# kv of six batches on two column halves of the matmul array, one head each, and one more batch's x on quarters

## The chip, the cores and the metric

One core of one Trainium2 chip runs the whole kernel. The metric is the device time of one execution in microseconds (us); lower is better. "Span" is the time from the first to the last instruction in a profile; it is some 1.8 us shorter than the device time.

Names as in the profile: PE is TensorE's matmuls, PEld its weight loads, DVE is VectorE, ACT is ScalarE, POOL is GpSimd. Of the program's names, pskv is the result of kv, psx and psxr are those of x (512 positions, and the other 64), psg and psv those of the up-projection (gate and value), psy that of the down-projection; xt and xtr are the copies of x, and ht the gated product, that the next matmuls read; yo is the output before it is stored.

## The reference

Linear attention over 8 batches, 8 heads, 576 positions, head size 64, followed by a gated feed-forward block over the 4608 tokens:

```python
q_s = softmax(q, axis=-1)                       # over the head dimension
k_s = softmax(k, axis=2)                        # over the sequence
kv  = np.einsum('bhsd,bhse->bhde', k_s, v)      # 64 x 64 per head
x   = np.einsum('bhsd,bhde->bhse', q_s, kv)     # then heads side by side: (4608, 512)
g   = x @ w_gate                                # 512 -> 1536
out = (gelu(g) * (x @ w_val)) @ w_out           # 1536 -> 512
```

Inputs and output are float32. The kernel computes in float16 with float32 sums.

## The kernel before

The feed-forward matmuls of one batch run on TensorE while the other engines prepare the next batch's attention. The small attention matmuls are slipped between the feed-forward matmuls by a plan: `at(b, FI, i, ...)` runs something after the i-th of twelve up-projection steps of batch b, and `at(b, NS, i, ...)` in its down-projection (0 to 3: after one of the four row blocks; 10 to 13: in the middle of one).

kv is computed for two heads at once on the whole array: the stationary weights are 128 columns of exp(k) (two heads), and the moving operand is v of the same two heads, each with a column of ones behind it (130 columns; the ones give the softmax sum). Half of the 128 x 130 result belongs to mismatched heads and is masked to zero:

```python
def kv_mm(b, g, j):
    ...
    hp = 2 * g + j
    for n in range(NC):                                            # NC = 5 chunks of positions
        nc.tensor.matmul(
            st[(b, "pskv", g)][:, j, :], ek_b[b % 2][:, n, hp * P:(hp + 1) * P],
            v16_b[b % 2][:, n, 2 * hp:2 * hp + 2, 0:VW],           # VW = 65
            start=(n == 0), stop=(n == NC - 1))

def kv_norm(b, g):
    pskv = st[(b, "pskv", g)]
    rck = att.tile([P, 2], f32, name="rck", tag="rck")
    nc.vector.reciprocal(out=rck, in_=pskv[:, :, D])
    for j in range(2):
        kv_sb = att.tile([P, 2, D], f16, name="kv_sb", tag="kv", bufs=12)
        nc.vector.scalar_tensor_tensor(                            # times 1/sum, times the mask
            out=kv_sb, in0=..., scalar=rck[:, j:j + 1], in1=mask, op0=ALU.mult, op1=ALU.mult)

def unit_kv(b, g):
    kv_mm(b, g, 0)
    kv_mm(b, g, 1)
    kv_norm(b, g)
```

For batches 3 to 7, x = q kv already runs on four 64x64 quarters of the array (`unit_x4`: row half s is one head's kv, column half t one of two head pairs). That needs heads h and h+4 side by side, which `exp` and `cast_v` arrange for batches from `T32 = 3` on. Batch 2 still uses the whole array (`unit_x`, four matmuls, and `unit_xrem`). The plan:

```python
at(1, NS, 0, L(unit_trem, 2), L(unit_kv, 2, 0))
at(1, NS, 1, L(unit_x, 2, 0, "dve"))
at(1, NS, 12, L(unit_kv, 2, 1))
at(1, NS, 2, L(unit_x, 2, 1, "dve"), L(unit_x, 2, 2, "dve"))
at(1, NS, 13, L(unit_x, 2, 3, "act"))
at(2, FI, 0, L(unit_xrem, 2, "dve"))
...
for b in range(2, B):                      # n = b + 1, batches 3 to 7
    ...
    at(b, FI, 5, L(unit_kv, n, 0))
    at(b, FI, 7, L(unit_kv, n, 1))
    at(b, NS, 1, L(unit_x4, n))
```

The softmax here doesn't subtract the row's maximum and nothing guards it: scores larger than these inputs give would overflow.

Of the kernel before, what the change touches and what calls it, by code (L numbers as in the profile page):

```python
# [9 lines left out]
f32 = mybir.dt.float32  # L10
f16 = mybir.dt.float16
ACTF = mybir.ActivationFunctionType
ALU = mybir.AluOpType
# [5 lines left out]
def kernel(  # L19
# [10 lines left out]
    nc = tc.nc  # L30

    B, H, S, D = q.shape
    C = H * D
    F = moe_w_gate.shape[1]
    P = 128
    HP = H // 2
# [6 lines left out]
    NC = NM + 1  # L43
    MAIN = NM * P
    REM = S - MAIN
    VW = D + 1
# [7 lines left out]
    att = ctx.enter_context(tc.tile_pool(name="att", bufs=2))  # L54
# [4 lines left out]
    ps_att = ctx.enter_context(tc.tile_pool(name="ps_att", bufs=2, space=bass.MemoryType.PSUM))  # L59
# [9 lines left out]
    ek_b, eq_b, v16_b = [], [], []  # L69
# [30 lines left out]



    T32 = 3

    def heads(x, b, h0, h1):

        if b >= T32:
            return x.rearrange("p (t c) x -> p c t x", t=2)[:, h0 // 2:h1 // 2]
        return x[:, h0:h1]

    tiles = {}
# [24 lines left out]
    def copy_on(eng, dst, src):  # L136
        if eng == "pool":
            nc.gpsimd.tensor_copy(out=dst, in_=src)  # L138
        elif eng == "act":
            nc.scalar.copy(out=dst, in_=src)  # L140
        else:
            nc.vector.tensor_copy(out=dst, in_=src)  # L142
# [14 lines left out]

    def exp(nm, b, h0=0, h1=H, n0=0):
        dst = (ek_b if nm == "k" else eq_b)[b % 2]
        o, i = (("p n (c t d) -> p c t n d", "p c t (n d) -> p c t n d") if b >= T32 else  # L160
                ("p n (h d) -> p h n d", "p h (n d) -> p h n d"))
        nc.scalar.activation(  # L162
            out=dst[:, n0:NC, h0 * D:h1 * D].rearrange(o, d=D, **({"t": 2} if b >= T32 else {})),
            in_=heads(tiles[(nm, b)], b, h0, h1)[..., n0 * D:NC * D].rearrange(i, d=D),
            func=ACTF.Exp)

    def cast_v(b, h0, h1, eng="pool"):
        if h1 - h0 > 2 and (eng == "pool" or b >= T32):
            for h in range(h0, h1, 2):
                cast_v(b, h, h + 2, eng)  # L170
            return
        copy_on(eng, v16_b[b % 2][:, :, h0:h1, 0:D].rearrange("p n h d -> p h n d"),
                (tiles[("v", b)][:, h0 // 2::4] if b >= T32 else tiles[("v", b)][:, h0:h1]).rearrange(
                    "p h (n d) -> p h n d", d=D))

    def norm_sum(b, hp, n0=0):
# [42 lines left out]
    st = {}  # L219
# [11 lines left out]
# [6 lines that stand above are left out]
            nc.vector.scalar_tensor_tensor(  # L237
                out=kv_sb,
                in0=pskv[:, j, :].rearrange("p (h e) -> p h e", e=VW)[:, :, 0:D],
                scalar=rck[:, j:j + 1], in1=mask, op0=ALU.mult, op1=ALU.mult)  # L240
            st[(b, "kv", 2 * g + j)] = kv_sb
# [29 lines left out]
    def unit_kv(b, g):  # L271
        kv_mm(b, g, 0)
        kv_mm(b, g, 1)
        kv_norm(b, g)

    def get_eqt(b):
        if (b, "eqt") not in st:
            st[(b, "eqt")] = att.tile([P, HP * 4 * NC * 32], f16, name="eqt", tag="eqt")[
                :, 0:HP * S].rearrange("p (h t) -> p h t", h=HP)
        return st[(b, "eqt")]  # L280

    def unit_t(b, g, eng="dve"):
        eqt = get_eqt(b)
        pst = ps_att.tile([P, 2, MAIN], f16, name="pst", tag="att")
        for j in range(2):
            hp = 2 * g + j
            for n in range(NM):
                nc.tensor.transpose(  # L288
                    pst[:, j, n * P:(n + 1) * P],
                    eq_b[b % 2][:, n + 1, hp * P:(hp + 1) * P], ident)  # L290
        st["evac_t"] = lambda eng: copy_on(eng, eqt[:, 2 * g:2 * g + 2, 0:MAIN], pst)
        if eng:
            st["evac_t"](eng)
# [33 lines left out]
    def xq(b, hp):  # L327

        if (b, "eqt5") in st:
            return st[(b, "eqt5")][:, hp, 1:NC]  # L330
        return st[(b, "eqt")][:, hp, 0:MAIN]

    def xqr(b, hp):
        if (b, "eqt5") in st:
            return st[(b, "eqt5")][:, hp, 0, :, 0:32:2]
        return st[(b, "eqtr")][:, hp, :]

    def get_xt(b):
        if (b, "xt") not in st:
            st[(b, "xt")] = att.tile([P, HP, MAIN], f16, name="xt", tag="xt")  # L340
        return st[(b, "xt")]
# [13 lines left out]
                             xqr(b, hp), start=True, stop=True)  # L355
        copy_on(eng, xtr[:, :, b * REM:(b + 1) * REM], psx)

    def unit_x4(b):

        xt = get_xt(b)  # L360

        def go(ps, hp, src):
            for s in range(2):
                r, t = slice(64 * s, 64 * s + 64), hp % 2
                nc.tensor.matmul(ps[s][64 * t:64 * t + 64], st[(b, "kv", hp)][r, s, :], src[r],  # L365
                                 start=True, stop=True)

        psr = [ps_att.tile([P, 2, REM], f32, name="psxr", tag="att") for _ in range(2)]
        for hp in range(HP):
            go([p[:, hp // 2] for p in psr], hp, xqr(b, hp))  # L370
        for s, eng in enumerate(("act", "dve")):
            copy_on(eng, xtr[:, 2 * s:2 * s + 2, b * REM:(b + 1) * REM], psr[s])
        for i in range(2):
            ps = [ps_big.tile([P, MAIN], f32, name="psx", tag="mm") for _ in range(2)]
            for hp in (2 * i, 2 * i + 1):
                go(ps, hp, xq(b, hp))
            for s, eng in enumerate(("act", "dve")):
                copy_on(eng, xt[:, i + 2 * s, :], ps[s])

    pswarm = ps_big.tile([P, 512], f32, name="pswarm", tag="mm")  # L380
# [160 lines left out]

    preload(ACTF.Exp)
    exp("q", 0, 0, 4, 1)
    exp("q", 0, 4, 8, 1)
    exp("k", 0, 0, 4)
    exp("k", 0, 4, 8)
    norm_pair(0, 0, 1, ("dve", "pool"))
# [7 lines left out]
    warm_pe(2)  # L555
    ksum_mm((2, 3))
    cast_v(0, 0, 2, "dve")
    cast_v(0, 2, 4, "act")
    ksum_rec()
    cast_v(0, 4, 6, "act")  # L560
    kv0_mm(0)
    kv0_mm(1)
# [23 lines left out]
    FI, NS = 0, 1  # L586
    plan = {}

    def at(b, kind, i, *fns):
        plan.setdefault((b, kind, i), []).extend(fns)  # L590

    L = lambda f, *a: (lambda: f(*a))
# [25 lines left out]
    at(1, FI, 9, L(unit_t, 2, 0))  # L618
    at(1, FI, 10, L(unit_t, 2, 1))
    at(1, FI, 11, L(load_batch, 3), L(exp, "k", 2, 4, 8), L(exp, "q", 3), L(exp, "k", 3), L(exp_rem0), L(cast_v, 3, 0, H))  # L620
    at(1, NS, 0, L(unit_trem, 2), L(unit_kv, 2, 0))
    at(1, NS, 1, L(unit_x, 2, 0, "dve"))
    at(1, NS, 12, L(unit_kv, 2, 1))
    at(1, NS, 2, L(unit_x, 2, 1, "dve"), L(unit_x, 2, 2, "dve"))
    at(1, NS, 13, L(unit_x, 2, 3, "act"))
    at(2, FI, 0, L(unit_xrem, 2, "dve"))
    at(2, FI, 7, L(norm_rem0))
    at(3, FI, 8, L(unit_trem, 0))
    at(3, FI, 11, L(unit_xrem, 0, "dve"))
    for b in range(2, B):  # L630
        if b + 2 < B:
            at(b, FI, 0, L(load_batch, b + 2))
            at(b, FI, NFI - 1, L(exp, "q", b + 2), L(exp, "k", b + 2), L(cast_v, b + 2, 0, H))
        if b + 1 < B:
            n = b + 1
            if n < T32:
                at(b, FI, 0, L(norm, n, 0))
                at(b, FI, 1, L(unit_kv, n, 0))
                at(b, FI, 2, L(norm, n, 1))
                at(b, FI, 3, L(unit_kv, n, 1))  # L640
                at(b, FI, 4, L(unit_t, n, 0), L(norm, n, 2))
                at(b, FI, 6, L(unit_x, n, 0), L(norm, n, 3))
                at(b, FI, 7, L(unit_x, n, 1))
                at(b, FI, 8, L(unit_t, n, 1))
                at(b, FI, 9, L(unit_trem, n))
                at(b, FI, 10, L(unit_x, n, 2), L(unit_x, n, 3))
                at(b, FI, 11, L(unit_xrem, n))
            else:
                for hp in range(HP):
                    at(b - 1, NS, hp, L(norm_sum, n, hp))  # L650
                    at(b, FI, hp, L(norm_mul, n, hp), L(unit_t32, n, hp))
                at(b, FI, 4, L(moves, n))
                at(b, FI, 5, L(unit_kv, n, 0))
                at(b, FI, 7, L(unit_kv, n, 1))
                at(b, NS, 1, L(unit_x4, n))


    def ride(b, kind, i):
# [68 lines left out]
```

## Time and profile before

| | before |
|---|---|
| device time, median (range) | 318.7 us (318.4 to 318.91, 3 runs) |
| span of the profiled run | 316.7 us |
| TensorE busy | 98% of the span |
| VectorE, ScalarE, GpSimd busy | 62%, 44%, 14% |
| kv matmuls on the whole array (L226) | 2% of the chain that ended last |

The busy shares say which engine can be the bound, not that it is. The chain of work that ended last and the waits say that. The prediction below shows these views and reads them. In all of them L226 is the source line; in a timeline line the first two numbers are start and duration in us, and the end of the line has the shape and the count. Durations of matmuls are modelled and overlap; only starts are used here.

### The profile page before, as it was taken

How to read it: one execution, taken by the hardware profiler on the slowest of the kernel's cores; microseconds unless marked ns; L12 is line 12 of the kernel's file. 1: busy time of each engine (PE TensorE's matmuls, PEld its weight loads, DVE VectorE, ACT ScalarE, POOL GpSimd, SP SyncE). 2: the span in 40 equal slices, each digit the busy share in tenths (PEclk: the TensorE clock that was granted, in tenths of full speed). 3: DMA queues.
4: the chain of work that ended last, by engine and by line, in shares of the span. 5: the costliest groups of instructions: out<-in, count | busy, mean ns of one | idle time of the engine just before them, and what ended most of it. 6: DMA issues, size and time to landing. Idle time of an engine off the chain costs nothing.

```text
span 316.7 us, 4572 instructions
## 1 busy us (share of the span) xinstructions
PE 309.7 (98%) x1698; PEld 146.8 (46%) x1698; DVE 195.4 (62%) x346; ACT 138.4 (44%) x179; POOL 44.6 (14%) x59
## 2 busy tenths in 40 slices
PE   8799999999999999999999999999999999999995
PEld 3444454455445444544444444444444444444444
DVE  3843386698898479847884689458953434234331
ACT  3753465989433663258233923392331233113300
POOL 2657551331003000110003000300000000000000
PEclk9999999999999999999999999999999999999999
DMA  7999999940196117821592149303020210140002
GB/s 229 372 383 395 400 386 388 394 174 0 68 321 236 45 66 251 291 56 68 169 364 63 55 122 382 97 10 132 3 63 23 91 42 2 27 105 2 2 33 99
DMA packets 42342, 50.76 MB, mean 160 GB/s; under 512 B 3408, under 2 KB 38096, under 8 KB 42320
## 3 DMA queue, kind: packets, MB, share of 16 engines
q1 hardware_dynamic: 40592, 48.84, 44.5%
q10 hardware_dynamic: 1728, 1.64, 1.6%
q8 instruction: 13, 0.21, 0.3%
q14 instruction: 9, 0.07, 0.1%
HBM read 37.75 MB, written 9.44 MB: 149 GB/s over the span
## 4 chain that ended last, share of the span: by engine, by line
PE 90%; DMA 4%; ACT 3%; DVE 2%; issue 1%; ACTq 0%
PE psy L471 29%; PE psg L393 28%; PE psv L393 28%; PE pskv L226 2%; DMA out_dram<-yo 2%; DMA qt<-in_q_dram 2%; PE psl L492 1%; DVE rq L190 1%; PE psx L365 1%; PE psx L347 1%; ACT eq L162 1%; PE pst L288 1%; DVE eq L199 0%; ACT L398 0%; ACT L162 0%
## 5 line engine op out<-in xcount | busy, mean ns | idle before, releaser
L398 ACT ACTIVATE gl<-psg 128x512 f32<-128x512 f32 x108 | 63.9, 598 | 141.4 <-PE psg L393 138.6
L400 DVE SCALAR_TENSOR_TENSOR ht<-psv,gl 128x512 f16<-128x512 f32 x108 | 72.9, 682 | 63.6 <-PE psv L393 63.0
L393 PE MATMUL psg<-xt,wg_sb 128*128 128x512 f16 x384 | 100.5, 379 | 0.1
L393 PE MATMUL psv<-xt,wv_sb 128*128 128x512 f16 x384 | 100.5, 379 | 0.0
L471 PE MATMUL psy<-wo_sb,ht 128*128 128x512 f16 x420 | 94.3, 379 | 0.0
L393 PEld LDWEIGHTS <-wv_sb 128*128 128x128 f16 x432 | 42.3, 98 | 51.2 <-issue 0.8
L393 PEld LDWEIGHTS <-wg_sb 128*128 128x128 f16 x432 | 41.6, 98 | 47.0 <-issue 0.4
L471 PEld LDWEIGHTS <-ht 128*128 128x128 f16 x420 | 40.4, 98 | 49.2 <-issue 2.1
L520 DVE TENSOR_SCALAR yo<-psy 128x512 f32<-128x512 f32 x30 | 20.6, 688 | 29.0 <-PE psy L471 29.0
L138 POOL CAST v<-vt 128x640 f16<-128x640 f32 x26 | 18.7, 761 | 137.5 <-DMA vt<-in_v_dram 92.2
L180 DVE TENSOR_REDUCE rq<-eq 128x10 f32<-128x640 f16 x28 | 22.7, 811 | 5.5 <-ACT eq L162 5.1
L199 DVE TENSOR_TENSOR eq<-eq,rrq 128x640 f16<-128x640 f16 (+1 forms) x29 | 23.4, 806 | 0.3
L162 ACT ACTIVATE ek<-kt 128x1280 f16<-128x1280 f32 (+1 forms) x11 | 19.1, 1746 | 3.4 <-DMA kt<-in_k_dram 3.4
L162 ACT ACTIVATE eq<-qt 128x2560 f16<-128x2560 f32 (+2 forms) x10 | 18.4, 1863 | 2.4 <-DMA qt<-in_q_dram 2.3
L313 DVE STREAM_TRANSPOSE et<-eq 128x640 f16<-128x640 f16 x20 | 16.9, 845 | 0.7
L140 ACT CAST xt<-psx 128x512 f16<-128x512 f32 x17 | 9.3, 589 | 7.4 <-PE psx L347 7.4
L393 PE MATMUL psg<-xtr,wg_sb 128*128 128x512 f16 x48 | 12.3, 379 | 0.0
L393 PE MATMUL psv<-xtr,wv_sb 128*128 128x512 f16 x48 | 12.3, 379 | 0.0
L385 PE MATMUL pswarm<-warm,ident 128*128 128x512 f16 x34 | 9.3, 430 | 1.4 <-POOL ident masks.py:199 1.4
L162 ACT ACT_TABLE_LOAD x8 | 10.3, 1283 | 0.7 <-DMA qt<-in_q_dram 0.6
L226 PEld LDWEIGHTS <-ek 128*128 128x128 f16 x140 | 9.1, 97 | 3.1
L142 DVE CAST xt<-psx 128x512 f16<-128x512 f32 x15 | 9.7, 681 | 1.2 <-PE psx L347 1.2
(70 smaller groups left out, 128.8 us busy)
## 6 DMA issues: line engine op xcount, KB each, us to landing
out_dram<-yo SPq DMA_DIRECT2D x14, 512.0 KB, 3.3
kt<-in_k_dram SPq DMA_DIRECT2D x7, 640.0 KB, 7.0
vt<-in_v_dram SPq DMA_DIRECT2D x7, 640.0 KB, 8.0
qt<-in_q_dram SPq DMA_DIRECT2D x7, 640.0 KB, 5.3
qt<-in_q_dram SPq DMA_DIRECT2D x8, 512.0 KB, 6.1
eqt<-et SPq DMA_DIRECT2D x80, 40.0 KB, 1.9
wost<-in_moe_w_out_dram SPq DMA_DIRECT2D x6, 512.0 KB, 7.9
kt<-in_k_dram SPq DMA_DIRECT2D x6, 512.0 KB, 7.5
```

The source lines that it names most:

```text
L138: nc.gpsimd.tensor_copy(out=dst, in_=src)
L142: nc.vector.tensor_copy(out=dst, in_=src)
L162: nc.scalar.activation(out=dst[:, n0:NC, h0 * D:h1 * D].rearrange(o, d=D, **({"t": 2} if b >= T32 else {})), in_=heads(tiles[(nm, b)], b, ...
L180: nc.vector.reduce_sum(rq, e, axis=mybir.AxisListType.X)
L199: (nc.gpsimd if eng == "pool" else nc.vector).tensor_tensor(out=e, in0=e, in1=rrq.unsqueeze(-1).to_broadcast((P, n, 2, D)), op=ALU.mult)
L226: nc.tensor.matmul(st[(b, "pskv", g)][:, j, :], ek_b[b % 2][:, n, hp * P:(hp + 1) * P], v16_b[b % 2][:, n, 2 * hp:2 * hp + 2, 0:VW], start ...
L313: nc.vector.transpose(out=et[:, :, hp].rearrange("p c (n i) -> p n c i", i=32), in_=eq_b[b % 2][:, :, hp * P:(hp + 1) * P].rearrange("p n ...
L393: nc.tensor.matmul(ps, w[:, ci, fi * P:(fi + 1) * P], xt[:, ci, :], start=(ci == 0), stop=(ci == HP - 1))
L398: nc.scalar.activation(out=gl, in_=psg, func=ACTF.Gelu)
L400: nc.vector.scalar_tensor_tensor(out=ht, in0=psv, scalar=_H_SCALE, in1=gl, op0=ALU.mult, op1=ALU.mult)
L471: nc.tensor.matmul(psy, hts[fi][:, ns * P:(ns + 1) * P], wo_sb[:, fi, :], start=(fi == 0), stop=(fi == NFI - 1))
L520: nc.vector.tensor_scalar(out=yo, in0=psy, scalar1=1.0 / _H_SCALE, scalar2=None, op0=ALU.mult)
```

## The change

Intent: a two-head kv matmul on the whole array computes twice what is needed. On two column halves (64 weight columns each), each half takes one head and streams only that head's 65 columns; the two halves are meant to work at the same time. All four head pairs of a batch go in one group, the result needs no mask, and one reciprocal and one multiply finish it. Batch 2 gets the head order of the later batches, so that its x too can go on quarters.

```diff
+    QUAD = 2
     T32 = 3
     def heads(x, b, h0, h1):
-        if b >= T32:
+        if b >= QUAD:
 # ... the same in exp and cast_v
+    def unit_kv4(b):
+        ps = ps_att.tile([P, HP, VW], f32, name="pskv", tag="att")
+        for hp in range(HP):
+            for n in range(NC):
+                for s in range(2):
+                    c0 = hp * P + s * D
+                    nc.tensor.matmul(
+                        ps[s * D:(s + 1) * D, hp, :], ek_b[b % 2][:, n, c0:c0 + D],
+                        v16_b[b % 2][:, n, 2 * hp + s, 0:VW], start=(n == 0), stop=(n == NC - 1))
+        rck = att.tile([P, HP], f32, name="rck4", tag="rck4")
+        nc.vector.reciprocal(out=rck, in_=ps[:, :, D])
+        kv = att.tile([P, HP, D], f16, name="kv4", tag="kv4")
+        nc.vector.tensor_tensor(out=kv, in0=ps[:, :, 0:D],
+                                in1=rck.unsqueeze(-1).to_broadcast((P, HP, D)), op=ALU.mult)
+        st[(b, "kv4")] = kv
-    def unit_x4(b):
+    def unit_x4(b, engs=("act", "dve")):
 # ... reads st[(b, "kv4")]; engs names the engines that copy x out
-    at(1, NS, 0, L(unit_trem, 2), L(unit_kv, 2, 0))
-    at(1, NS, 1, L(unit_x, 2, 0, "dve"))
-    at(1, NS, 12, L(unit_kv, 2, 1))
-    at(1, NS, 2, L(unit_x, 2, 1, "dve"), L(unit_x, 2, 2, "dve"))
-    at(1, NS, 13, L(unit_x, 2, 3, "act"))
-    at(2, FI, 0, L(unit_xrem, 2, "dve"))
+    at(1, NS, 0, L(unit_trem, 2))
+    at(1, NS, 1, L(unit_kv4, 2))
+    at(1, NS, 2, L(unit_x4, 2, ("dve", "dve")))
 # ... batches 3 to 7 (a branch for n < T32 that never ran is dropped as well)
-                at(b, FI, 5, L(unit_kv, n, 0))
-                at(b, FI, 7, L(unit_kv, n, 1))
+            at(b, FI, 5, L(unit_kv4, n))
```

More of the change, by code (lines that the diff above doesn't have):

```diff
@@ L159, in exp @@
         dst = (ek_b if nm == "k" else eq_b)[b % 2]
-        o, i = (("p n (c t d) -> p c t n d", "p c t (n d) -> p c t n d") if b >= T32 else
+        o, i = (("p n (c t d) -> p c t n d", "p c t (n d) -> p c t n d") if b >= QUAD else
                 ("p n (h d) -> p h n d", "p h (n d) -> p h n d"))
         nc.scalar.activation(
-            out=dst[:, n0:NC, h0 * D:h1 * D].rearrange(o, d=D, **({"t": 2} if b >= T32 else {})),
+            out=dst[:, n0:NC, h0 * D:h1 * D].rearrange(o, d=D, **({"t": 2} if b >= QUAD else {})),
             in_=heads(tiles[(nm, b)], b, h0, h1)[..., n0 * D:NC * D].rearrange(i, d=D),
@@ L167, in cast_v @@
     def cast_v(b, h0, h1, eng="pool"):
-        if h1 - h0 > 2 and (eng == "pool" or b >= T32):
+        if h1 - h0 > 2 and (eng == "pool" or b >= QUAD):
             for h in range(h0, h1, 2):
@@ L172, in cast_v @@
         copy_on(eng, v16_b[b % 2][:, :, h0:h1, 0:D].rearrange("p n h d -> p h n d"),
-                (tiles[("v", b)][:, h0 // 2::4] if b >= T32 else tiles[("v", b)][:, h0:h1]).rearrange(
+                (tiles[("v", b)][:, h0 // 2::4] if b >= QUAD else tiles[("v", b)][:, h0:h1]).rearrange(
                     "p h (n d) -> p h n d", d=D))
@@ L364, in go @@
                 r, t = slice(64 * s, 64 * s + 64), hp % 2
-                nc.tensor.matmul(ps[s][64 * t:64 * t + 64], st[(b, "kv", hp)][r, s, :], src[r],
+                nc.tensor.matmul(ps[s][64 * t:64 * t + 64], st[(b, "kv4")][r, hp, :], src[r],
                                  start=True, stop=True)
@@ L370, in unit_x4 @@
             go([p[:, hp // 2] for p in psr], hp, xqr(b, hp))
-        for s, eng in enumerate(("act", "dve")):
+        for s, eng in enumerate(engs):
             copy_on(eng, xtr[:, 2 * s:2 * s + 2, b * REM:(b + 1) * REM], psr[s])
@@ L376, in unit_x4 @@
                 go(ps, hp, xq(b, hp))
-            for s, eng in enumerate(("act", "dve")):
+            for s, eng in enumerate(engs):
                 copy_on(eng, xt[:, i + 2 * s, :], ps[s])
@@ L635 @@
             n = b + 1
-            if n < T32:
-                at(b, FI, 0, L(norm, n, 0))
-                at(b, FI, 1, L(unit_kv, n, 0))
-                at(b, FI, 2, L(norm, n, 1))
-                at(b, FI, 3, L(unit_kv, n, 1))
-                at(b, FI, 4, L(unit_t, n, 0), L(norm, n, 2))
-                at(b, FI, 6, L(unit_x, n, 0), L(norm, n, 3))
-                at(b, FI, 7, L(unit_x, n, 1))
-                at(b, FI, 8, L(unit_t, n, 1))
-                at(b, FI, 9, L(unit_trem, n))
-                at(b, FI, 10, L(unit_x, n, 2), L(unit_x, n, 3))
-                at(b, FI, 11, L(unit_xrem, n))
-            else:
-                for hp in range(HP):
-                    at(b - 1, NS, hp, L(norm_sum, n, hp))
-                    at(b, FI, hp, L(norm_mul, n, hp), L(unit_t32, n, hp))
-                at(b, FI, 4, L(moves, n))
-                at(b, FI, 5, L(unit_kv, n, 0))
-                at(b, FI, 7, L(unit_kv, n, 1))
-                at(b, NS, 1, L(unit_x4, n))
+            for hp in range(HP):
+                at(b - 1, NS, hp, L(norm_sum, n, hp))
+                at(b, FI, hp, L(norm_mul, n, hp), L(unit_t32, n, hp))
+            at(b, FI, 4, L(moves, n))
+            at(b, FI, 5, L(unit_kv4, n))
+            at(b, NS, 1, L(unit_x4, n))
     def ride(b, kind, i):
```

## The prediction

> **What bounds the kernel now.** I first read the page's engine totals and its 40 slices, then the chain that ended last, then TensorE's waits, and last the order of time around the instructions that the change touches. First the page, engine totals and two rows of its slices:
>
> ```profile
> PE 309.7 (98%) x1698; PEld 146.8 (46%) x1698; DVE 195.4 (62%) x346; ACT 138.4 (44%) x179; POOL 44.6 (14%) x59
> ...
> PE   8799999999999999999999999999999999999995
> ...
> DMA  7999999940196117821592149303020210140002
> ```
>
> TensorE is busy in every slice. The transfers are near full only in the first nine slices (about 71 us); the first instruction that the change touches after the loads, batch 2's kv, starts at 75.7 us. A busy TensorE row alone proves little, because ends of matmuls are modelled, so I read the chain (page) and TensorE's waits (whole span):
>
> ```profile
> PE psy L471 29%; PE psg L393 28%; PE psv L393 28%; PE pskv L226 2%; DMA out_dram<-yo 2%; DMA qt<-in_q_dram 2%; PE psl L492 1%; DVE rq L190 1%; PE psx L365 1%; PE psx L347 1%; ACT eq L162 1%; PE pst L288 1%; DVE eq L199 0%; ACT L398 0%; ACT L162 0%
> ```
> ```profile
> PE pswarm L385 <- POOL ident masks.py:199: 1.4, 1, 1.4
> PE pst L288 <- DVE eq L199: 0.7, 1, 0.7
> PE pskv L260 <- DVE v L142: 0.4, 1, 0.4
> PE pst L288 <- POOL eq L199: 0.4, 1, 0.4
> PE psx L347 <- DVE kv_sb L266: 0.2, 1, 0.2
> ```
>
> All five waits lie in the first 15 us; from 60 us to the end the waits view names none for TensorE. So after 60 us the time is the sum of TensorE's start-to-start steps, and only a change in these steps, or a new wait, moves the end. The kv matmuls (L226) are 2% of the chain: that is all there is to win from, and not all of it can go.
>
> **What a kv unit and a quarter-array x cost today.** In order of time, TensorE only, around one kv unit (two head pairs, ten matmuls) and around one x of a later batch, which already runs on 64x64 quarters:
>
> ```profile
> 95.94 0.74 PE L226 MATMUL pskv<-v,ek 128*128 128x130 f16 x10
> 96.51 0.38 PE L393 MATMUL psg<-xt,wg_sb 128*128 128x512 f16 x1
> ```
> ```profile
> 112.41 0.38 PE L471 MATMUL psy<-wo_sb,ht 128*128 128x512 f16 x1
> 112.72 0.26 PE L365 MATMUL psxr<-eqt,kv_sb 64*64 64x64 f16 x8
> 112.81 0.39 PE L365 MATMUL psx<-eqt,kv_sb 64*64 64x512 f16 x4
> ```
> ```profile
> 113.02 0.39 PE L365 MATMUL psx<-eqt,kv_sb 64*64 64x512 f16 x4
> 113.34 0.82 PE L471 MATMUL psy<-wo_sb,ht 128*128 128x512 f16 x3
> ```
>
> I use starts, not durations. The kv unit holds the array from 95.937 to 96.512: 0.575 us, or 57.5 ns per matmul of 130 columns. Two units per batch: **1.15 us**. A full-array matmul of 512 columns steps by 216 ns. In the quarter-array x the single records give, in ns after the start of the psy matmul before it: eight 64-column matmuls in two groups of four at 309 and 361, then groups of 512 columns at 396 and 612, and the next psy at 931, with 226 to the one after. All five x units repeat this within 4 ns. So:
> - going in costs 309 - 216 = 93 ns, and coming out 931 - 612 - 213 = 106 ns plus 10 ns in the next step: **about 0.21 us for a visit** to another tiling;
> - four matmuls on different quarters start 3 to 4 ns apart, and groups of 64 columns follow at 52 ns (the first) and then 32 to 35 ns.
>
> **What the Trainium skill says.** (1) "TensorEngine Tiling (Array Packing)", section "Key Properties": changing the tiling mode drains TensorE, and tiles load weights and multiply in parallel. The trace agrees: 93 and 116 ns at the borders, starts 3 to 4 ns apart. (2) "TensorE: Matmul & The Clock Gate", section "Wait — 56ns, not 53.3ns?": a warm step is N / 2.4 GHz plus about 2.5 ns; for 130 columns 56.7, the trace has 57.5; for 65 columns it makes 29.6 ns (estimate). (3) The same page, section "LDWEIGHTS (loading the stationary operand)", gives a load as columns / 1.2, 53 ns for 64 columns, and the tiling page says under "Restrictions" that column tiling switches Fast Weight Load off. The trace of the quarters differs from 53: groups of 64-column loads start at 112.718, 112.747, 112.775 and 112.809, 28 to 34 ns apart. The measurement decides for me, though it is for 64 rows and not 128. (4) The tiling page, "Instruction Overhead", puts about 60 cycles (25 ns at 2.4 GHz) on each matmul. The twenty one-column matmuls of L249 mostly step by 25 ns, but the quarters show that this does not add up across tiles.
>
> **The change, part by part.**
> 1. *kv of batches 2 to 7.* Removed: 20 matmuls of 128x130 per batch, half of whose result was masked to zero. Added: 40 of 128x65, alternating between two column halves, in one visit. Twenty pairs; with the pitch of the quarters, 32 ns (load of 64 columns about 27, then the start; above the 29.6 of the 65 columns themselves). Cost of a visit: entry 0.093 + first step's extra 0.02 + 19 x 0.032 = 0.608 + last pair 0.027 + exit 0.116 = **0.86 us**. Against 1.15: 0.29 saved per batch, x 6 = **1.7 us**. Had the columns alone counted, half of 1.15 would go, 3.4 us in all; the visit's borders take 1.3 of this.
> 2. *x of batch 2.* Before: four steps of 216 ns and four remainders that took 87.187 to 87.303, together 0.98 us. After: one x visit as in later batches, 931 - 216 + 10 = 0.73 us. **0.25 us** saved.
> 3. *VectorE.* Per batch two reciprocals (156 ns) and four masked multiplies (347) become one reciprocal and one multiply of 128x256 (estimate 0.42 us, from the 128x256 cast out of the array's result buffer, 0.415): about 1.1 us less, beside TensorE. It is worth nothing on the path, as TensorE never waits there.
> 4. *Batch 2's layout* (heads paired h and h+4) moves the same bytes through the same number of exps and casts; the later batches' 4 x 0.8 us casts on POOL show no dearer form. Nothing on the path.
> 5. *Batch 2's x is all copied by VectorE,* in one go: two of 0.28 and four of 0.68 us, where before ScalarE took one and the rest was spread out.
>
> Sum: 1.7 + 0.25 = 2.0 us of 318.7, so **316.7 us**, 0.6% faster.
>
> **The rivals.**
> - *VectorE's burst stalls batch 2's first up-projection.* Counted from the last psy start before x: yo copy at 0.42, xtr copies at 1.02 and 1.22, xt copies from 1.42 every 0.60 (as the pairs at 83.03 and 83.63 do), so the last, chunk 3, ends at 3.9. The up-projection starts at 0.93 + 12 x 0.216 = 3.5, needs chunk 1 at 3.75 (ready 3.3) and chunk 3 at 4.18. Margin 0.28 us. After it, gates run about 1 us later than now: the worst, fi 4, which starts 2.6 us after its last psv matmul now, would reach 3.4, where the fourth later psv needs its buffer at about 3.8. So I expect no stall; if I missed a step it costs 0.1 to 0.5 us, once.
> - *The halves do not overlap their weight loads as the quarters do.* A load of 64 columns over 128 rows, without the fast mode, at 53 ns: pitch about 58, a visit 1.36 us, 0.21 lost per batch, total 1.0 us slower: 319.7. Against it stand the measured 28 to 34 ns and the fact that each partition feeds the same two streams in quarters and in halves. I give it 1 in 8.
> - *Fully serial halves* (40 x 53 ns): 2.3 us a visit, 7 us lost, 325 us. Nothing speaks for it but the page; 1 in 50.
> - *A better pitch*, 28 ns: 0.78 a visit, 2.5 us saved, 316.2.
> - *Leaving full rows takes longer to drain than quarters:* some 30 ns per visit, 0.2 us in all.
>
> **Range and chances.** 316.7 as the centre; 28 ns pitch and a little luck give 315.9; a pitch of 40 ns (a visit of 1.0 us) with a stall of 0.5 us saves 0.15 x 6 + 0.25 - 0.5 = 0.65 us, 318.05. I take 315.9 to 318.4, which leaves out the 1 in 8 above. Faster by over 2% would need 6.4 us, more than what can be halved; slower by over 2% needs the serial case.
>
> **What would show it.** In the changed trace, kv's 40 matmuls should start in pairs a few ns apart, pairs 32 ns apart; the visit from entry to the next full-array matmul should add 0.86 us (0.76 to 0.95), with 93 and 106 ns at its borders. Batches 3 to 6 should have a period of 32.66 us where 32.95 stands now. Batch 2's x should add 0.73 us, and TensorE should show no wait after 60 us. VectorE busy should fall by 6 to 7 us. I am wrong if pairs step by 50 ns or more, if the two halves start one after the other, if the borders cost more than 0.3 us, or if a wait of TensorE for xt or for a psv buffer appears at 83 to 95 us.

## The result, and the profile after

The changed kernel took 316.76 us (median of 4 runs, 316.35 to 317.13) against 318.75 us of the kernel before (4 runs, 318.4 to 318.91). The ratio is 0.9939 with a 95% interval of 0.9922 to 0.9956: 0.6% faster. A repeat of the unchanged source later gave 0.9942.

The page's engine totals and its chain by line, after:

```profile
PE 308.4 (98%) x1826; PEld 143.4 (46%) x1826; DVE 190.8 (61%) x324; ACT 137.8 (44%) x178; POOL 44.6 (14%) x59
...
PE psy L489 29%; PE psg L411 27%; PE psv L411 27%; DMA out_dram<-yo 2%; DMA qt<-in_q_dram 2%; PE pskv L284 1%; DVE eq L200 1%; PE psl L510 1%; PE psx L383 1%; DVE rq L191 1%; DVE rq L181 1%; DVE ht L418 1%; ACT eq L163 1%; PE pst L306 0%; ACT L416 0%
```

TensorE has more instructions, is still busy 98% of the span, and still carries the chain; kv (now L284) fell from 2% to 1% of it. TensorE's waits from 60 us on, where the kernel before had none:

```profile
PE pst L306 <- DVE eq L200: 0.3, 1, 0.3
```

That single wait is at 71 us, before any TensorE instruction that the change moves; it is taken up below. Around one kv visit, and around batch 2's x, in order of time, TensorE only:

```profile
95.55 0.38 PE L411 MATMUL psv<-xt,wv_sb 128*128 128x512 f16 x1
95.86 0.25 PE L284 MATMUL pskv<-v,ek 128*64 128x65 f16 x4
```
```profile
95.86 0.82 PE L284 MATMUL pskv<-v,ek 128*64 128x65 f16 x40
96.61 0.39 PE L411 MATMUL psg<-xt,wg_sb 128*128 128x512 f16 x1
```
```profile
82.18 0.25 PE L383 MATMUL psxr<-eqt,kv 64*64 64x64 f16 x8
82.27 0.60 PE L383 MATMUL psx<-eqt,kv 64*64 64x512 f16 x8
82.81 0.39 PE L489 MATMUL psy<-wo_sb,ht 128*128 128x512 f16 x1
```

The form 128*64 is the column half. From the records one by one, in ns after the start of the last full-array matmul: the pairs start at 309 and 312, 361 and 364, 397 and 400, ... 932 and 935, and the next full-array matmul starts at 1064, followed by one at 225 instead of 216. The visit adds 1064 - 216 + 9 = 0.857 us; the six visits give 0.857 to 0.859. Batch 2's x adds 0.725 us.

Busy time of each engine in one whole batch period (from batch 4's first up-projection matmul to batch 5's); the kernel before, then the changed one:

```profile
151.99:184.95 32.96, 32.96 (x182) 15.39 (x180) 23.43 (x41) 15.42 (x19) 2.72 (x4) 1.00 0.47 160
```
```profile
151.24:183.90 32.66, 32.66 (x201) 14.85 (x200) 22.57 (x37) 15.42 (x19) 2.72 (x4) 1.00 0.48 162
```

The columns are the stretch, its length, busy us and instruction count of PE, PEld, DVE, ACT and POOL, then the clock, the DMA share and GB/s. PE fills the stretch in both; the stretch itself is 0.29 us shorter.

### The profile page after: what moved, and what is told of

It reads as the page before. It is cut to its first block, busy times and chain, and to the rows that moved or that the text cites. A ratio compares the mean times of both kernels' runs of the same rounds, so it can differ in the third digit from the quotient of the medians.

```text
span 315.0 us, 4799 instructions
## 1 busy us (share of the span) xinstructions
PE 308.4 (98%) x1826; PEld 143.4 (46%) x1826; DVE 190.8 (61%) x324; ACT 137.8 (44%) x178; POOL 44.6 (14%) x59
## 4 chain that ended last, share of the span: by engine, by line
PE 87%; DMA 4%; DVE 4%; ACT 3%; issue 1%; ACTq 0%; DVEq 0%
PE psy L489 29%; PE psg L411 27%; PE psv L411 27%; DMA out_dram<-yo 2%; DMA qt<-in_q_dram 2%; PE pskv L284 1%; DVE eq L200 1%; PE psl L510 1%; PE psx L383 1%; DVE rq L191 1%; DVE rq L181 1%; DVE ht L418 1%; ACT eq L163 1%; PE pst L306 0%; ACT L416 0%
## 5 line engine op out<-in xcount | busy, mean ns | idle before, releaser
L418 DVE SCALAR_TENSOR_TENSOR ht<-psv,gl 128x512 f16<-128x512 f32 x108 | 72.9, 682 | 66.3 <-PE psv L411 65.7
```

Of the source, the lines that this page charges most:

```text
L418: nc.vector.scalar_tensor_tensor(out=ht, in0=psv, scalar=_H_SCALE, in1=gl, op0=ALU.mult, op1=ALU.mult)
```

## The experiments

Two numbers from the trace tell the kernels apart better than the total: the **period** (from one batch's x visit to the next) and the **tail**, the time from batch 1's first down-projection matmul, just ahead of every TensorE instruction that the change touches, to the end of the span. What lies before it took 72.6 to 73.4 us in the profiles, and the changed kernel alone gave 73.2 and 73.0. Only batch 2's new head order (its exps and casts) lies in that stretch: it averages 73.0 us in the eleven profiles with it and 72.9 in the three without, and batch 2's four casts of v take 2.72 us before and after, so it shows no cost. The tail repeats within 5 ns between runs of kernels with the same work on TensorE.

| kernel | kv per batch on TensorE, us | period, us | tail, us | median, us | ratio to before |
|---|---|---|---|---|---|
| before | 1.15 | 32.956 | 243.80 | 318.75 | |
| changed | 0.858 | 32.664 | 241.81 | 316.76 | 0.9939 |
| changed_again | 0.858 | 32.664 | 241.81 | 316.58 | 0.9942 |
| halves_3to7 | 0.858 | 32.664 | 242.36 | 316.92 | 0.9951 |
| batch2_only | 1.15 | 32.956 | 243.26 | 318.10 | 0.9987 |
| two_visits | 2 x 0.542 | 32.890 | 243.17 | 318.11 | 0.9985 |
| full_one_group | 1.15 | 32.956 | 243.81 | 318.81 | 1.000 |
| vector_ballast | 0.859 | 32.664 | 241.81 | 316.69 | 0.9934 |
| narrow_columns | 0.845 | 32.651 | 241.72 | 316.58 | 0.9931 |
| one_half_at_a_time | 0.917 | 32.723 | 242.15 | 317.17 | 0.9956 |
| one_half_then_other | 1.39 | 33.197 | 244.99 | 319.85 | 1.0044 |
| same_half | 1.490 | 33.297 | 245.60 | 320.26 | 1.0059 |
| merged_visit | 0.753 | 32.558 | 241.39 | 315.89 | 0.9911 |

The experiments ran in three groups; each ratio is against runs of the kernel before on the same chip (medians 318.63, 318.75 and 318.38). All ratios are within 2% of 1; what tells the kernels apart is the intervals given below and, more sharply, the tails.

### Each part alone: halves_3to7 and batch2_only

```diff
 # halves_3to7, against the changed kernel
-    QUAD = 2
+    QUAD = 3          # and batch 2's plan lines of the kernel before
```
```diff
 # batch2_only, against the changed kernel
-            at(b, FI, 5, L(unit_kv4, n))
+            at(b, FI, 5, L(unit_kv, n, 0))
+            at(b, FI, 7, L(unit_kv, n, 1))
 # and unit_x4 reads the old kv_sb tiles for b > 2
```

> Only kv of batches 3 to 7 on column halves; batch 2 as in the kernel before. Theory (array time of the visits): 5 visits of 0.858 us instead of 5 x 1.15, so 1.46 us less than before: about 317.3 us, ratio to before 0.9954. Batch period 32.66 us as in the changed kernel. Rival (the gain comes from batch 2's new x and layout): within 0.2 us of before, ratio 0.9995.

> Only batch 2 changed (one kv visit, x on quarters), batches 3 to 7 as before. Theory: 0.29 + 0.25 = 0.54 us less than before, about 318.2 us, ratio 0.9983, periods of later batches 32.95 us. Rival (batch 2 is what matters): 1.5 us or more less, ratio 0.9953 or lower.

Measured: 0.9951 (0.9938 to 0.9963) and 0.9987 (0.9975 to 1.0000). In the tail, halves_3to7 saves 1.45 us and batch2_only 0.54; the sum is 1.99, and the whole change saves 1.99. So the two parts do not help or hinder each other, and about three quarters of the gain is kv of batches 3 to 7.

### Grouping and VectorE: full_one_group and vector_ballast

```diff
 # full_one_group, against the kernel before
-                at(b, FI, 5, L(unit_kv, n, 0))
-                at(b, FI, 7, L(unit_kv, n, 1))
+                at(b, FI, 5, L(unit_kv, n, 0), L(unit_kv, n, 1))
```
```diff
 # vector_ballast, against the changed kernel (the kv pool cut from 12 to 10 buffers for room)
         st[(b, "kv4")] = kv
+        for j in range(4):
+            dum = att.tile([P, 2, D], f16, name="dum", tag="dum")
+            nc.vector.scalar_tensor_tensor(
+                out=dum, in0=ps[:, 2 * (j % 2):2 * (j % 2) + 2, 0:D],
+                scalar=rck[:, j:j + 1], in1=mask, op0=ALU.mult, op1=ALU.mult)
```

> Kernel before, with the two kv units of batches 3 to 7 back to back in one place (full array, 130 columns, as before). Theory (only array time counts): 20 x 57.5 ns in either arrangement, no change, ratio 1.000, period 32.95 us. Rival (part of the gain comes from making one group of two): 0.5 us or more less than before, ratio 0.998 or lower.

> Changed kernel with four masked multiplies of 128x128 on VectorE after each kv, whose results nobody uses: 4 x 0.35 = 1.4 us per batch, more than the 1.1 us that the change took off VectorE. Theory (VectorE is off the path): as the changed kernel, ratio to before 0.994, period 32.66 us. Rival (the lighter VectorE is part of the gain): some or all of the gain lost, ratio 0.997 to 1.000.

Measured: 1.000 (0.9987 to 1.0014), tail 243.81 as before; and 0.9934 (0.9921 to 0.9946), tail 241.81 as the changed kernel. Joining two groups into one is worth nothing on the whole array. Giving VectorE back the work that the change took from it costs nothing; the same batch period as above, vector_ballast:

```profile
150.73:183.40 32.67, 32.67 (x202) 14.86 (x200) 23.52 (x41) 15.43 (x19) 2.73 (x4) 1.00 0.48 162
```

VectorE is back at 23.5 us busy, where it was before the change, and the period stays. Both rivals fall.

### What a visit's borders cost: two_visits

```diff
-    def unit_kv4(b):
+    def unit_kv4(b, g):                      # two head pairs per call
 # ...
-            at(b, FI, 5, L(unit_kv4, n))
+            at(b, FI, 5, L(unit_kv4, n, 0))
+            at(b, FI, 7, L(unit_kv4, n, 1))
 # batch 2: at (1, NS, 0) and (1, NS, 1)
```

> Halves as in the changed kernel, but each batch's kv in two visits of 10 pairs instead of one of 20. Theory (a visit has a fixed cost at its borders): a visit of 10 pairs costs 0.858 - 10 x 0.030 = 0.556 us, two 1.11; against 1.15 on the full array 0.04 saved per batch; with batch 2's x 0.5 us less than before: 318.3 us, ratio 0.9985, period 32.91 us. Rival (the borders are free or small, the columns alone count): as the changed kernel, 316.8 us, ratio 0.994.

Measured: 0.9985 (0.9971 to 0.9999), period 32.890. One of the two visits, TensorE only:

```profile
95.76 0.51 PE L285 MATMUL pskv<-v,ek 128*64 128x65 f16 x20
96.20 0.39 PE L412 MATMUL psg<-xt,wg_sb 128*128 128x512 f16 x1
```

A visit of 10 pairs costs 0.542 us, a little under the 0.556 expected, because the pairs are 31.7 ns apart and not the 30.2 that I put in: 0.858 - 10 x 0.0317 = 0.541. So a visit is 10 x 0.0317 = 0.317 us of pairs and **0.225 us that does not depend on their number**: 93 ns going in, about 100 + 9 coming out, and some 20 for a first pair that takes longer. Splitting the group throws away almost the whole kv gain (0.066 of 0.292 us per period is left). This is why the group of four pairs is part of the idea, though grouping alone is worth nothing.

### What sets 32 ns per pair: narrow_columns

```diff
-                        ps[s * D:(s + 1) * D, hp, :], ek_b[b % 2][:, n, c0:c0 + D],
-                        v16_b[b % 2][:, n, 2 * hp + s, 0:VW], ...
+                        ps[s * D:(s + 1) * D, hp, 32:VW], ek_b[b % 2][:, n, c0:c0 + D],
+                        v16_b[b % 2][:, n, 2 * hp + s, 32:VW], ...
 # the multiply behind it reads these 32 columns of the result twice
```

> Changed kernel with each kv matmul streaming 33 columns instead of 65 (wrong result on purpose). Theory A (the pitch of the pairs is set by loading 64 columns of weights): pairs stay 29 to 31 ns apart, a visit stays at 0.84 to 0.86 us, time as the changed kernel (316.8). Theory B (the pitch is set by the 65 streamed columns): pairs about 16 ns apart[...], a visit about 0.57 us, 1.7 us less in all: 315.1.

The result was wrong, as intended. In its order of time, TensorE only:

```profile
96.00 0.81 PE L284 MATMUL pskv<-v,ek 128*64 128x33 f16 x40
96.74 0.39 PE L412 MATMUL psg<-xt,wg_sb 128*128 128x512 f16 x1
```

Streaming half the columns left the visit at 0.845 us. From the second pair to the twentieth is 570 ns in both kernels (361 to 931 here, 361 to 932 in the changed kernel): 31.7 ns per pair. The 13 ns saved are those of the last pair, 32 columns fewer (estimate from the Trainium skill's 2.4 GHz, "TensorE: Matmul & The Clock Gate", section "Wait — 56ns, not 53.3ns?": 13.3). So Theory B falls: the pitch is not that of streaming 65 columns. Theory A, that loading 64 columns of weights sets it, fits the order of the records (in same_half below, nearly every load starts 1 to 3 ns after the matmul before it, and its own matmul follows 25 to 34 ns after the load), but it is not shown: no run changed the number of weight columns, so a fixed step per matmul on a half would look the same. The "29 to 31 ns" of the expectation was a misreading on my side of the changed kernel's records, which have 31.7 too.

### Do the halves overlap: one_half_at_a_time, which_half, one_half_then_other, same_half

```diff
 # one_half_at_a_time
-            for n in range(NC):
-                for s in range(2):
+            for s in range(2):
+                for n in range(NC):
```

> Changed kernel with the two loops swapped: five matmuls on one half, then five on the other, same instructions, one visit. Theory (the gain is the overlap of the two halves): matmuls 30 ns apart one by one, 40 x 0.030 + 0.25 = 1.46 us a visit, 0.6 more than the changed kernel in each of six batches: 320.4 us, ratio to before 1.005. Rival (the halves win because each matmul is short and the result smaller, not because they overlap): as the changed kernel, ratio 0.994.

**This expectation missed.** With five matmuls on one half and then five on the other, a visit costs 0.917 us, only 0.06 more than with alternating ones (six times that is the growth of the tail, 0.34 us):

```profile
95.89 0.88 PE L284 MATMUL pskv<-v,ek 128*64 128x65 f16 x40
96.71 0.39 PE L411 MATMUL psg<-xt,wg_sb 128*128 128x512 f16 x1
```

Its records show starts about 18 ns apart on average, so two halves were running, although neighbours in the program were on the same half. To see which, the second half's matmuls were given a 66th column (a spare column of ones, the result unchanged):

```diff
 # which_half, against one_half_at_a_time (the result tile is one column wider too)
-        nc.gpsimd.memset(v16_b[i][:, :, :, D:D + 1], 1.0)
+        nc.gpsimd.memset(v16_b[i][:, :, :, D:D + 2], 1.0)
 # ...
-                        ps[s * D:(s + 1) * D, hp, :], ek_b[b % 2][:, n, c0:c0 + D],
-                        v16_b[b % 2][:, n, 2 * hp + s, 0:VW], ...
+                        ps[s * D:(s + 1) * D, hp, 0:VW + s], ek_b[b % 2][:, n, c0:c0 + D],
+                        v16_b[b % 2][:, n, 2 * hp + s, 0:VW + s], ...
```

> The order of one_half_at_a_time, with the second half's matmuls made recognisable (66 columns, a spare column of ones, result unchanged). That run missed its expectation (a visit of 0.918 us, not 1.46). Theory A (TensorE starts matmuls of the other half ahead of programme order): the first 66-column matmul starts within 70 ns of the first 65-column one, before the third 65-column one; visit about 0.92 us. Theory B (programme order holds): the first 66-column matmul starts after all five of the first half, 120 ns or more after the first.

The time (316.88 us) is one run of unknown state and is not used; the order is. The first records of one visit, read one by one from the trace (not a view of the profile), ns from its first weight load; program order is five of 65 columns, then five of 66:

```
  0 load    2 matmul 65
 29 load   54 matmul 65
 57 load   (for the third 65)
 59 load   60 matmul 66     <- sixth in the program
 87 load   90 matmul 65
 92 load  113 matmul 66 ...
```

The sixth matmul of the program starts 58 ns after the first, ahead of the third. Theory A holds: TensorE starts a matmul of the free half ahead of waiting ones of the busy half. How far ahead it looks was asked with all 20 of one half before all 20 of the other:

```diff
 # one_half_then_other, against which_half
-        for hp in range(HP):
-            for s in range(2):
+        for s in range(2):
+            for hp in range(HP):
```

> All 20 matmuls of one half, then all 20 of the other. Theory A (TensorE looks some tens of instructions ahead): the halves still overlap in good part, visit below 1.1 us, time below 318.2. Theory B (it reaches only about the ten instructions that one_half_at_a_time needed): 20 x 31.7 one after the other twice, visit 1.4 to 1.5 us, time about 320.3, ratio to before 1.005.

Measured: 1.0044 (1.0031 to 1.0058), a visit of 1.39 us: Theory B. In its records the first 66-column weight load starts at 537 ns, right behind the seventeenth 65-column matmul (533), with three 65-column matmuls (562, 596 and 625) still to come. In which_half the first came with three to come as well. So in both orders the reach is **three matmuls and their loads**, not the whole group. Finally, everything on the first half:

```diff
 # same_half, against one_half_at_a_time (wrong result on purpose)
-                        ps[s * D:(s + 1) * D, hp, :], ek_b...
+                        ps[0:D, hp, :], ek_b...
 # rows 64 to 127 of kv are set to zero
```

> All 40 matmuls of a visit on the first half of the array (wrong result on purpose), so that nothing can overlap. Theory (the gain is the overlap of the two halves): 40 x 31.7 + 0.23 = 1.50 us a visit, 0.64 more than the changed kernel in each of 6 batches: 320.6 us, ratio to before 1.006. Rival (short matmuls and short weights alone give the gain): as the changed kernel, 0.994.

```profile
96.38 1.45 PE L284 MATMUL pskv<-v,ek 128*64 128x65 f16 x40
97.77 0.39 PE L412 MATMUL psg<-xt,wg_sb 128*128 128x512 f16 x1
```

Measured: 1.0059 (1.0045 to 1.0073), a visit of 1.490 us, 40 matmuls 32 ns apart. The same matmuls without overlap are slower than the whole array's 1.15 us. So the overlap of the halves is what makes the gain: without it a visit costs 0.63 us more.

### A version that beats both: merged_visit

If a visit's borders are a quarter of its cost, two visits should share one. kv of batches 4 to 7 goes right behind the x of the batch before it:

```diff
-            at(b, FI, 5, L(unit_kv4, n))
-            at(b, NS, 1, L(unit_x4, n))
+            if n == 3:
+                at(b, FI, 5, L(unit_kv4, n))
+            at(b, NS, 2, L(unit_x4, n), *([L(unit_kv4, n + 1)] if n + 1 < B else []))
 # pskv of batches 4 to 7 comes from the larger pool of result buffers
```

> Changed kernel with kv of batches 4 to 7 put right behind the x of the batch before, so that quarters are followed by halves without full-array matmuls between. Theory A (each switch of tiling costs some 0.1 us): two borders of about 0.1 us go in each of 4 batches and one comes, 0.4 us less than the changed kernel: 316.4 us, ratio to before 0.9926. Theory B (only going between full array and tiles costs): 4 x 0.21 = 0.84 us less: 315.9, ratio 0.991. Rival: a new wait in the busy stretch between two batches eats it: 0.994 or above.

```profile
147.12 0.26 PE L384 MATMUL psxr<-eqt,kv 64*64 64x64 f16 x8
147.21 0.60 PE L384 MATMUL psx<-eqt,kv 64*64 64x512 f16 x8
147.74 0.82 PE L285 MATMUL pskv<-v,ek 128*64 128x65 f16 x40
148.50 0.39 PE L490 MATMUL psy<-wo_sb,ht 128*128 128x512 f16 x1
```

The joint visit costs 1.478 us, against 0.725 + 0.858 = 1.583 apart: 0.105 saved. In single records the last x group starts at 612 to 622 ns after the matmul before the visit, and such groups follow each other by 216; the first kv matmul follows at 928, so going from quarters to halves costs about 100 ns, one border like the others. Four joint visits shorten the tail from 241.81 to 241.39: 0.42 us, where Theory A said 0.4 and Theory B 0.84. So by the trace it is Theory A. By the total alone it would have been B: the measured ratio, 0.9911 (0.9898 to 0.9925), is what B said, and its interval just misses A's 0.9926. But of the 0.87 us between the medians of this kernel and the changed one (315.89 and 316.76, from different rounds) only 0.42 is in the tail as traced, and the stretch before the tail differs by 0.7 us among the other profiles.

### The stretch before 73 us: changed_again

The changed kernel as it is, once more.

> The changed kernel itself once more. From the start of batch 1's down-projection to the end 241.81 us as in its first profile (241.81), while the 73 us before vary by up to 0.8 us between profiles with a wait of TensorE for VectorE near 71 us that comes and goes: so ratio to before 0.993 to 0.995, and the merged visit (0.9911) is 0.13% (0.42 us) better by its trace.

Measured: 0.9942 (0.9928 to 0.9955); the tail is 241.81 again, and no wait after 60 us. The wait at 71 us is thus not part of the changed kernel as such. It also shows in batch2_only, narrow_columns and one_half_at_a_time (0.2 to 0.3 us), and in full_one_group, whose batch 2 is that of the kernel before. Where it occurs in the changed kernel, a normalising multiply on VectorE took longer than in the kernel before, while GpSimd cast v in both (first line before, second the changed kernel):

```profile
69.92 0.92 DVE L199 TENSOR_TENSOR eq<-eq,rrq 128x640 f16<-128x640 f16 x1
```
```profile
69.84 1.38 DVE L200 TENSOR_TENSOR eq<-eq,rrq 128x640 f16<-128x640 f16 x1
```

What makes it take longer in some executions was not tried. The 0.38 us by which batch 1's down-projection started later in this profile is why the profiled spans differ by 1.6 us while the tails differ by 2.0.

## Why the prediction was right

- *The bound.* It named the sum of TensorE's start-to-start steps after 60 us. The tails show it: 243.80 to 241.81, 1.99 us, where the sum said 2.0. full_one_group and vector_ballast exclude grouping and VectorE.
- *kv.* A visit was put at 0.86 us with a pitch of 32 ns; measured 0.858 and 31.7. The terms held singly as well: entry 93, exit about 100 + 9 (predicted 106 + 10). Of its reason for the pitch, narrow_columns shows one part, that the streamed columns do not set it; the other, that the weight load does, is not shown. The rival that leaving full rows takes longer to drain than leaving quarters fell: both exits are about 100 ns. The period was predicted at 32.66 us and measured at 32.664.
- *The disagreement with the skill's load time.* The prediction took the 28 to 34 ns of the quarters' loads over 53 ns from the page. Loads of 64 columns over 128 rows, which no trace had shown, kept the same step (31.7 ns); the rival with 58 ns pairs fell.
- *x of batch 2.* 0.73 us predicted, 0.725 measured; batch2_only saves 0.54, as 0.29 + 0.25 said.
- *VectorE's burst.* It was the rival that came closest, and the predicted sequence can be checked line by line, VectorE in order of time:

```profile
82.29 0.69 DVE L538 TENSOR_SCALAR yo<-psy 128x512 f32<-128x512 f32 x1 [1.07 <-PE psy L489]
82.90 0.48 DVE L143 CAST xtr<-psxr 128x128 f16<-128x128 f32 x2
83.30 2.47 DVE L143 CAST xt<-psx 128x512 f16<-128x512 f32 x4
85.69 0.81 DVE L181 TENSOR_REDUCE rq<-eq 128x10 f32<-128x640 f16 x1
```

  The last xt copy ends at 85.77; the matmul that needs it starts at 86.05. The predicted margin was 0.28 us, and this is 0.28. The gate product of the fifth up-projection step (fi 4) started 3.1 us after its last psv matmul, where the prediction put 3.4 against a limit of 3.8, and TensorE did not wait. The shift of the gates was overrated: this one went from 2.6 to 3.1 us, not by "about 1". The limit was too strict as well: the pool of psg and psv has six buffers, so, taken in turn, fi 4's is next written by fi 7's psv, which started 5.4 us after fi 4's last.
- *What was off.* VectorE's busy time fell by 4.6 us, not 6 to 7. The prediction added durations of instructions that overlap at their ends (two multiplies of 0.35 us lasted 0.61 together), and left out in its count that a copy of x moved over from ScalarE; the slower multiply at 71 us adds little, as changed_again, without it, fell by 4.8. As VectorE is off the path, none of this reached the time. And what I said of the halves in the expectations, that swapped loops would make them serial, was wrong: TensorE looked three matmuls ahead in both orders tried. TensorE was also to show no wait after 60 us; the 0.3 us at 71 us is one, though changed_again has none.
- *What was luck.* The median came within 0.06 us of the centre, closer than the first 73 us let any total be known; what bears out the sum is the tail and the single terms.

## What to carry to other kernels

A small matmul that fills only part of the array's result can go on column halves, but the gain is the overlap, and each visit to another tiling costs a fixed 0.2 us: put as many small matmuls as possible into one visit, and let visits share a border. Compute the cost of a visit as borders plus pairs times the step of one pair, both read as start-to-start steps from a trace that already has a tiled stretch. Where one engine's steps are the time, compare kernels by a stretch of the trace that starts after the varying part; it settled here 0.1 us where medians vary by 0.5.

## What the Trainium skill lacked or had wrong

- "TensorE: Matmul & The Clock Gate", Part 3, section "The mechanism", states that matmuls start in program order without reordering. On column halves they do not: in which_half the sixth matmul of the program started 58 ns after the first and ahead of the third. The reach was three matmuls in both orders tried (one_half_then_other: 1.39 us a visit, almost serial).
- The same page, same section, lists that weight loads overlap matmuls in flight only where the row group differs, though its paragraph above also allows loads into a background buffer. The "only" is too narrow: on column halves, which share all rows, a load for the second half started at 59 ns (which_half), 5 ns after a matmul of the first half and 31 ns before that half's next. Whether that used the background buffer no run shows.
- The same page, section "LDWEIGHTS (loading the stationary operand)": 64 columns come to 53 ns by its formula. The runs show a load and the start of its matmul every 31.7 ns, with 33 or 65 streamed columns, on 128 rows and without overlap of another half (same_half: 32 ns).
- "TensorEngine Tiling (Array Packing)", section "Key Properties", says that a change of tiling mode drains TensorE but gives no cost: 93 ns from the whole array to tiles, about 110 back, and about 100 from quarters to halves; 0.225 us per visit with the slower first pair.
